# An mLSTM cell and a gated MLP on one core: gates of four chunks at once, and half passes in the second chunk

## The chip, the cores and the metric

The kernel runs on 1 core of one Trainium2 chip. The metric is the device time of one execution in microseconds (us), smaller is better. "TensorE" (PE in the profile) multiplies matrices, "VectorE" (DVE), "ScalarE" (ACT) and "GpSimd" (POOL) work element by element, and SP only issues transfers; ScalarE and GpSimd issue some as well. Each of them works off its own queue in order.

## The reference, cut to what matters

```python
# attention: batch 4, heads 8, sequence S = 768, head size D = 40
for t in range(S):
    m_new = np.maximum(f_gate[:, :, t] + m, i_gate[:, :, t])
    f_stab = np.exp(f_gate[:, :, t] + m - m_new)
    i_stab = np.exp(i_gate[:, :, t] - m_new)
    m = m_new
    C = f_stab[..., None, None] * C + i_stab[..., None, None] * outer(v_t, k_t)
    n = f_stab[..., None] * n + i_stab[..., None] * k_t
    y[:, :, t] = sigmoid(o_gate_t) * (C @ q_t) / np.maximum(np.abs(n @ q_t), 1.0)
# then an MLP on x = y as (3072, 320):  w_in (320, 2048), w_out (2048, 320)
h = x @ w_in
out = (h / (1 + np.exp(-1.702 * h))) @ w_out
```

All data are float32.

## The kernel before

**Chunks.** The sequence is cut into NW = 6 chunks (w = 0 to 5) of L = 128 steps. A chunk's attention works on all 32 pairs of batch and head (BH) at once; its result is 512 rows (4 batches x 128 steps) of 320 features for the MLP. The program is one stream of calls in a hand-made order: for each w an *up* stage (x @ w_in in 8 pairs j of 128-wide feature blocks), then a *down* stage (the product with w_out), into which the attention of chunk w + 1 is woven block by block (`attention`, the dictionary `side`). A pool's tag with `bufs` buffers hands them out in turn; a tile that takes a buffer waits for whoever still uses it.

**The gates.** `gates(w)` runs on VectorE, on 32 partitions: a running sum of f, a running maximum, and what has to be exponentiated later, with the two halves of the chunk swapped for odd heads by the masks `odd` and `even`. Each chunk starts from the maximum that the chunk before left (`m_at`). `load_gates` (two loads) comes before it; `gates_out` stores the results to DRAM in five transfers, `columns_in` fetches them back in five as columns, and `spread` fetches the running maximum once for all 128 partitions into two `wt` tiles. `side_queue` says who issues: GpSimd for chunk 1, SP for the others. `gates(1)` stands in the up stage of chunk 0 after pair j = 3, `gates(2)` in that of chunk 1 after j = 0, the later ones in down stages (i == 7).

**The up stage and its terms.** From chunk 1 on, a float32 product is made of rounded parts: `x_high`, `x_low`, `x_diff` against `w_high`, `w_low`, `w_diff`, for the first 256 features (k = 0, 1), in two sums, `main` and `side`. The last 64 features are in `x_rest` and `w_rest`. In chunks 2 to 5 `up_strips` does this in half passes: `halves` gives two matmuls of 64 rows each, one for each block of the pair, on the two halves of the array, so that both run together. There the last 64 features take one term `both` (high and low parts on the two halves) and one `strip`, half as much. A half pass that would write a sum while its other half is still on its way waits for a mark: `seen` puts an empty instruction into ScalarE's queue that waits for a matmul, and the next matmul waits for it. Chunk 1 uses `up_fast`: whole passes of 128 rows, eight terms for each block, two of them for the last 64 features, and no marks.

**Around it.** `evict_side` (ScalarE) and `evict_main` (VectorE) empty the sums, `gelu_fast` (ScalarE) follows. During the up stage of chunk 1 the parts of w_in that the later chunks need are also made (`split_high` on ScalarE, `split_diff` and `split_low` on VectorE) and stored to DRAM by `keep`, on ScalarE's queue. `keep_last` copies the last of them to another buffer. `weight_sums`, `hidden_difference` and `hidden_sums` (GpSimd, the last two pairs on VectorE) prepare the down stage, which from chunk 1 on takes seven products of sums instead of eight. `half_sums` and `wait_for` (a one-column copy to `mark`) hold GpSimd back until a given tile is written. `count` adds increments of a semaphore that nobody waits for to the first `COUNTS[w]` passes of a stage.

Of the kernel before, what the change touches and what calls it, by code (L numbers as in the profile page):

```python
# [8 lines left out]
FP = mybir.dt.float32  # L9
# [16 lines left out]
COUNTS = {0: 54, 1: 128, 2: 105, 3: 105}  # L26
# [9 lines left out]
def kernel(  # L36
# [178 lines left out]
    one1 = const.tile([BH, 1], FP, name="one1")  # L215
# [3 lines left out]
    ones = one1.to_broadcast([BH, L])  # L219
# [9 lines left out]
    odd, even = (const.tile([3 * BH, 1], FP, name=n) for n in ("odd", "even"))  # L229
# [10 lines left out]
    cols, stacked, m_row, raw = {}, {}, {}, {}  # L240
# [61 lines left out]
    def gates(w):  # L302
# [30 lines left out]
        if w:  # L333
            for x in range(2):
                V.tensor_scalar(out=swapped[:, x * HL:(x + 1) * HL], in0=st[:, (1 - x) * HL:(2 - x) * HL], scalar1=odd,
                                scalar2=None, op0=OP.mult)
            V.scalar_tensor_tensor(out=swapped, in0=st, scalar=even, in1=swapped, op0=OP.mult, op1=OP.add)
# [4 lines left out]

    def gates_out(w):
        m_run, swapped, both = stacked[w]
        to = m_row[w] = rows.tile([2, BH, HL], FP, name="m_row")
        side_queue(w).dma_start(out=to[:, 0::2].rearrange("n h t -> h n t"),
                          in_=m_run[0::2].rearrange("h (n t) -> h n t", t=HL))
        for n in range(2):
            side_queue(w).dma_start(out=to[1 - n, 1::2], in_=m_run[1::2, n * HL:(n + 1) * HL])
        st_row = rows.tile([L // 32, 3 * BH, 32], FP, name="st_row")  # L350
        d_row = rows.tile([BH, 2], FP, name="d_row")
        stacked[w] = st_row, d_row
        side_queue(w).dma_start(out=st_row.rearrange("n k t -> k n t"), in_=swapped.rearrange("k (n t) -> k n t", t=32))
        side_queue(w).dma_start(out=d_row, in_=both)
# [11 lines left out]
    def masks():  # L366
        V.tensor_reduce(out=odd, in_=full.rearrange("p (j two) -> p two j", two=2)[:, 1], axis=AX.X, op=OP.add)
        V.memset(odd[BH:2 * BH, :], 0.0)
        V.tensor_scalar(out=even, in0=odd, scalar1=-1.0, scalar2=1.0, op0=OP.mult, op1=OP.add)

    def columns_in(w):
# [3 lines left out]
        for n in range(L // 32):  # L375
            side_queue(w).dma_start(out=x[n * 32:n * 32 + 32, 0:3 * BH].rearrange("r (k t) -> r k t", t=32),
                              in_=st_row[n].rearrange("(k r) t -> r k t", r=BH))
# [46 lines left out]
    def spread(w):  # L424

        for c in range(2):
# [281 lines left out]
    w_high, w_low, w_diff, w_rest = {}, {}, {}, []  # L708
# [11 lines left out]
    def by_strips(w):  # L720
        return w > 1

    def rooms(w):
# [4 lines left out]
        if w > 1:  # L728
            w_low.update({(w, n): gp.tile([128, 2, 512], FR, tag="g", name="w_low")
                          for n in ((2, 3) if by_strips(w) else (2,))})  # L730
# [4 lines left out]
    def more_rooms(w):  # L735

        w_low[w, 3], w_diff[w, 2], w_low[w, 2], w_diff[w, 3] = (gp.tile([128, 2, 512], FR, tag="g", name=name)
                                                                for name in ("w_low", "w_diff", "w_low", "w_diff"))
# [18 lines left out]
    def keep_last():  # L757
        w_low[3] = work.tile([128, 2, 512], FR, tag="wx", bufs=1, name="w_low")
        A.copy(out=w_low[3], in_=w_low.pop((1, 3)))

# [15 lines left out]

    def strip_weights():

        wr = w_rest[0]
        w_rest.append(work.tile([128, NF // 2, 128], FR, tag="wx", bufs=1, name="w_strip"))  # L780
        d, low, high = w_rest[1], wr[64:128], wr[0:64]
# [12 lines left out]
    def split_x(w, c):  # L794
# [9 lines left out]
        A.activation(out=x_rest[w][0][:, t], in_=x[:, 2], func=AF.Copy, scale=BIAS if by_strips(w) else -BIAS / BASE)  # L804
# [9 lines left out]
    def split_x_rest(w, c):  # L814
        t, x = part_of(w, c)
        both, other = x_rest[w]
        if by_strips(w):
            V.scalar_tensor_tensor(out=other[:, t], in0=both[:, t], scalar=-1.0 - 1.0 / BASE, in1=x[:, 2], op0=OP.mult,
                                   op1=OP.add)
        else:  # L820
            V.scalar_tensor_tensor(out=other[:, t], in0=x[:, 2], scalar=-1.0 / BASE, in1=both[:, t], op0=OP.mult,
                                   op1=OP.subtract)
# [6 lines left out]
    def split_on(w):  # L829
# [5 lines left out]
        if by_strips(w):  # L835
# [12 lines left out]
    def up_fast(w, j):  # L848
# [33 lines left out]
        if j:  # L882
            gelu_fast(w, j - 1)
# [535 lines left out]
```

## Time and profile before

| | us |
|---|---|
| median of 3 runs | 438.51 (437.26 to 439.23) |
| the profiled execution | 438.98 |
| its span in the profile | 437.3 |
| TensorE busy | 431.9 |
| VectorE busy | 353.5 |
| ScalarE busy | 247.2 |
| GpSimd busy | 146.7 |

The granted clock of TensorE is 1.00 throughout. A line of the timeline has the start, the duration, the engine, the line of the kernel, the operation, output and inputs with their sizes, how many instructions are merged, and in brackets how long the engine had stood idle and what ended that. In the chain of waits each line is the start, the length and what the chain was then in.

### The profile page before, as it was taken

The page shows a single profiled execution, that of the slowest core. Times are in us where ns is not written, and L with a number is a line of the kernel's source. Part 1 is how long each engine was busy: PE and PEld are TensorE (multiplying, and loading weights), DVE is VectorE, ACT ScalarE, POOL GpSimd, SP SyncE. Part 2 cuts the span into 40 slices and gives each one's busy share as a digit, 9 for nine tenths or more (in the row PEclk, how much of TensorE's full clock was granted, in tenths as well). Part 3 has the DMA queues.
Part 4 walks back from the last instruction along what each step waited for, and adds up shares of the span by engine and source line. Part 5 has one row for each costly group of instructions (what it writes and reads, how often), then busy time and mean ns, then how long its engine had stood idle before and what let it go on. Part 6 is the DMA issues. An engine that isn't in the chain of part 4 may idle for free.

```text
span 437.3 us, 13451 instructions
## 1 busy us (share of the span) xinstructions
PE 431.9 (99%) x5342; PEld 375.0 (86%) x5342; DVE 353.5 (81%) x689; ACT 247.2 (57%) x540; POOL 146.7 (34%) x155
## 2 busy tenths in 40 slices
PE   8999999999999999999999999999999999999996
PEld 6877887777888999888999888999887999888996
DVE  4898998989889799659789659789759759779990
ACT  5677779922777900397900386900287940298720
POOL 6411326533056822035712035622036624013100
PEclk9999999999999999999999999999999999999999
DMA  8999999217797516999306997605998925820000
GB/s 169 188 285 193 254 252 225 66 34 186 198 206 152 127 49 156 312 161 172 54 31 146 311 178 154 86 19 131 282 197 151 121 66 125 258 98 2 0 32 30
DMA packets 130733, 64.07 MB, mean 147 GB/s; under 512 B 102208, under 2 KB 122672, under 8 KB 130672
## 3 DMA queue, kind: packets, MB, share of 16 engines
q1 hardware_dynamic: 121232, 57.48, 59.4%
q10 hardware_dynamic: 8768, 4.28, 3.4%
q0 software_dynamic: 672, 1.46, 1.2%
q8 instruction: 43, 0.70, 0.7%
q14 instruction: 18, 0.15, 0.1%
HBM read 51.86 MB, written 11.34 MB: 145 GB/s over the span
## 4 chain that ended last, share of the span: by engine, by line
PE 94%; ACT 2%; DVE 1%; DMA 1%; issue 0%; SPq 0%; DVEq 0%
PE p_out L1036 26%; PE p_h L911 13%; PE p L911 10%; PE p_out L979 8%; PE p_h L663 7%; PE p L1114 5%; PE p L865 3%; PE p_h L865 3%; PE p L931 3%; PE p L540 2%; PE p L548 2%; PE p L496 2%; PE p_h L673 2%; PE p_out L1114 2%; PE p L639 2%; PE p L412 1%
## 5 line engine op out<-in xcount | busy, mean ns | idle before, releaser
L803 ACT ACTIVATE x_high<-xT 128x512 fp32r<-128x512 f32 x10 | 6.3, 631 | 88.4 <-DVE xT L609 88.4
L1036 PE MATMUL p_out<-w_out,g 128*128 128x160 f32 x384 | 55.5, 301 | 0.0
L1036 PEld LDWEIGHTS p_out<-w_out,g 128*128 128x128 f32 x384 | 52.9, 190 | 1.6 <-ACT g L966 1.3
L843 ACT ACTIVATE g<-g 128x512 f32<-128x512 f32 x80 | 45.7, 629 | 1.9 <-DVE g L971 1.6
L1004 POOL TENSOR_TENSOR g<-g 128x512 f32<-128x512 f32 x16 | 20.5, 1302 | 69.9 <-ACT g L843 63.1
L971 DVE SCALAR_TENSOR_TENSOR g<-p,g 128x512 f32<-128x512 f32 x40 | 25.7, 684 | 22.5 <-PE p L911 19.2
L966 ACT ACTIVATE g<-p 128x512 f32<-128x512 f32 x40 | 21.7, 596 | 34.9 <-PE p L911 29.8
L469 ACT ACTIVATE wt<-wt,cols 128x64 f32<-128x64 f32 x160 | 38.9, 335 | 0.1
L1036 PE MATMUL p_out<-t_sb,s 128*128 128x160 f32 x256 | 37.8, 301 | 0.0
L1036 PEld LDWEIGHTS p_out<-t_sb,s 128*128 128x128 f32 x256 | 35.5, 190 | 0.2
L979 PE MATMUL p_out<-w_out,g 128*128 128x320 f32 x128 | 35.7, 436 | 0.0
L971 DVE SCALAR_TENSOR_TENSOR g<-p_h,g 128x512 f32<-128x512 f32 x40 | 25.7, 687 | 11.9 <-PE p_h L911 11.9
L979 PEld LDWEIGHTS p_out<-w_out,g 128*128 128x128 f32 x128 | 24.0, 190 | 9.5
L1021 POOL TENSOR_TENSOR s<-g,s 128x256 f32<-128x256 f32 x16 | 12.9, 835 | 52.8 <-PE p_out L1036 52.8
L663 PE MATMUL p_h<-xT,w_in 128*128 128x256 f32 x128 | 29.8, 385 | 0.1
L663 PEld LDWEIGHTS p_h<-xT,w_in 128*128 128x128 f32 x128 | 23.6, 190 | 5.4 <-issue 2.2
L966 ACT ACTIVATE g<-p_h 128x512 f32<-128x512 f32 x40 | 21.6, 593 | 10.3 <-PE p_h L911 9.2
L476 POOL TENSOR_SCALAR_AFFINE_SELECT wt<-wt 64x1024 f32<-64x1024 f32 x20 | 24.3, 1214 | 6.9 <-ACT wt L469 6.0
L625 POOL TENSOR_TENSOR vw<-v_st,cols 128x656 f32<-128x656 f32 (+1 forms) x13 | 16.7, 1301 | 25.0 <-PE p_out L1036 15.4
L1041 DVE TENSOR_TENSOR o_sb<-o_sb,p_out 128x160 f32<-128x160 f32 x56 | 16.3, 314 | 9.7 <-PE p_out L1036 9.2
L421 DVE STREAM_TRANSPOSE qT<-q_sq 128x512 f32<-128x512 f32 x20 | 20.4, 1109 | 1.2 <-ACT q_sq L122 1.2
L911 PE MATMUL p_h<-x_diff,w_diff 64*128 64x512 f32 x128 | 20.3, 395 | 0.0
(260 smaller groups left out, 1097.2 us busy)
## 6 DMA issues: line engine op xcount, KB each, us to landing
w_diff<-w_row SPq DMA_DIRECT2D x16, 512.0 KB, 4.8
wt<-m_row SPq DMA_DIRECT2D x20, 256.0 KB, 5.3
bits<-in_moe_w_in_dram SPq DMA_DIRECT2D x8, 512.0 KB, 9.5
w_low<-w_row SPq DMA_DIRECT2D x8, 512.0 KB, 6.2
out_dram<-o_sb SPq DMA_DIRECT2D x24, 160.0 KB, 2.9
q_sq<-in_q_dram SPq DMA_DIRECT2D x10, 320.0 KB, 8.1
eo<-in_o_gate_dram SPq DMA_DIRECT2D x5, 640.0 KB, 7.4
bits<-in_moe_w_out_dram SPq DMA_DIRECT2D x8, 320.0 KB, 5.4
```

What stands on the lines that cost most here:

```text
L469: A.activation(out=x[:, h, :], in_=x[:, h, :], func=AF.Exp, scale=-1.0, bias=cols[w][:, c * PH + h:c * PH + h + 1])
L476: G.affine_select(out=r, in_=r, compare_op=OP.is_ge, fill=0.0, base=0, pattern=[[0, PH], [1, HL]], channel_multiplier=-1)
L663: T.matmul(ph[j][i][:, t], w_in[f // 4][:, c, f % 4 * 128:f % 4 * 128 + 128], x[:, c, t], start=(first and c == 0 and n == 0), stop=(not f ...
L843: A.activation(out=g, in_=g, func=AF.Gelu_apprx_sigmoid)
L865: T.matmul(dst[i], a(i), x, start=(first and m == which[0]), stop=(last and m == which[-1]))
L911: mm = T.matmul(to[f], a(f)[r], x[r], start=(first and n == 0), stop=(last and n + 1 == len(parts)))
L966: A.activation(out=g[:, i, :], in_=opened[w, j][0][i], func=AF.Copy, scale=-BASE)
L971: V.scalar_tensor_tensor(out=g[:, i, :], in0=opened[w, j][1][i], scalar=1.0 + 1.0 / BASE, in1=g[:, i, :], op0=OP.mult, op1=OP.add)
L979: T.matmul(po, gs[w, f // 2][:, f % 2, b * L:(b + 1) * L], w_out_sb[f // NH][:, f % NH, :], start=(f == 0), stop=(f == NF - 1))
L1004: G.tensor_tensor(out=a10, in0=a00, in1=a10, op=OP.subtract)
L1036: T.matmul(po, a(f), b[:, f, :], start=(f == 0), stop=(f == NH - 1))
L1114: T.matmul((main, side, main)[n], g_part[n, b, f // 2][:, f % 2], wo[n, f][0][:, wo[n, f][1]], start=(f == order[0] and n < 2), stop=(f == ...
```

## The change

The gates of chunks 1 to 4 are loaded together into one tile of 128 partitions by eight loads in GpSimd's queue (`load_four`, during the attention of chunk 0), and worked out together on VectorE where `gates(1)` stood (`gates_four`); the maximum is carried from one chunk to the next in four one-column steps. GpSimd stores chunk 1's results, SP stores those of chunks 2 to 4 in the down stage of chunk 0 (`four_out`). `gates` is left for chunk 0 and chunk 5. Chunk 1's up stage becomes `up_strips`, with marks of GpSimd in pairs 0 to 4 and of ScalarE afterwards. Its `strip` weights are made on VectorE before the stage (`first_strip`, in a `wt` buffer), `x_rest` gets one more step on VectorE, the gelus come later, the last `w_low` gets a buffer of the pool `sp` and is stored by ScalarE's queue without the copy, and the second half of chunk 2's `spread` comes after pair 7. `COUNTS[1]` goes from 128 to 154, and products of the down stage are counted too.

```diff
-COUNTS = {0: 54, 1: 128, 2: 105, 3: 105}
+COUNTS = {0: 54, 1: 154, 2: 105, 3: 105}
...
+    def load_four():
+        x = work.tile([L, 768], FP, tag="y", name="gates4")
+        four["in"] = [x[:, n * L:(n + 1) * L] for n in range(4)]
+        for n, src in enumerate((f_gate, i_gate)):
+            for x in range(4):
+                G.dma_start(out=four["in"][n][x * BH:(x + 1) * BH],
+                                  in_=src[:, :, (x + 1) * L:(x + 2) * L].rearrange("b h s -> (b h) s"))
+
+    def gates_four():
+        f, i, f_run, m_run = four["in"]
+        x = work.tile([L, 768], FP, tag="y", name="gates4")
...
+        V.tensor_tensor_scan(out=f_run, data0=ones4, data1=f, initial=0.0, op0=OP.mult, op1=OP.add)
+        V.tensor_tensor(out=a, in0=i, in1=f_run, op=OP.subtract)
+        V.tensor_tensor_scan(out=m_run, data0=ones4, data1=a, initial=NEG, op0=OP.mult, op1=OP.max)
+        V.tensor_copy(out=m[0:BH], in_=m_at[1])
+        for n in range(4):
+            r = slice(n * BH, (n + 1) * BH)
+            V.scalar_tensor_tensor(out=m[(n + 1) * BH:(n + 2) * BH] if n < 3 else m_at[NW - 1], in0=m_run[r, L - 1:L],
+                                   scalar=m[r], in1=f_run[r, L - 1:L], op0=OP.max, op1=OP.add)
+        V.tensor_scalar(out=m_run, in0=m_run, scalar1=m, scalar2=None, op0=OP.max)
...
-        w_low[w, 3], w_diff[w, 2], w_low[w, 2], w_diff[w, 3] = (gp.tile([128, 2, 512], FR, tag="g", name=name)
-                                                                for name in ("w_low", "w_diff", "w_low", "w_diff"))
+        w_low[w, 3] = sp.tile([128, 2, 512], FR, tag="g", name="w_low")
+        w_diff[w, 2], w_low[w, 2], w_diff[w, 3] = (gp.tile([128, 2, 512], FR, tag="g", name=name)
+                                                   for name in ("w_diff", "w_low", "w_diff"))
...
+    def first_strip():
+        w_strip[1] = work.tile([128, NF // 2, 128], FR, tag="wt", bufs=2, name="w_strip")
+        V.scalar_tensor_tensor(out=w_strip[1], in0=rest_high, scalar=-1.0 / BASE, in1=rest_low, op0=OP.mult, op1=OP.add)
...
-        if by_strips(w):
-            both, other = x_rest[w]
-            V.scalar_tensor_tensor(out=both[64:128], in0=other[64:128], scalar=BASE, in1=both[64:128], op0=OP.mult,
-                                   op1=OP.add)
+        both, other = x_rest[w]
+        V.scalar_tensor_tensor(out=both[64:128], in0=other[64:128], scalar=BASE, in1=both[64:128], op0=OP.mult, op1=OP.add)
...
-        note = (A if w + 1 < NW else nc.sync).nop()
+        note = (nc.sync if w + 1 == NW else G if w == 1 and j < 5 else A).nop()
...
-        late = j < 3 and w + 1 < NW
-        for n in ((), (), (0, 1))[j] if late else (j - 1,) if w + 1 < NW or j + 1 < NF // 2 else ():
+        late = {1: (), 2: (), 3: (0, 1), 4: (2,), 5: (3,), 6: (4, 5)} if w == 1 else {1: (), 2: (0, 1)} if w + 1 < NW else {7: ()}
+        for n in late.get(j, (j - 1,)):
...
+    load_four()
+    load(1, "k")
...
-                    gates(1)
-                    gates_out(1)
+                    gates_four()
+                    four_out(G, 1, 2)
...
-                (up_strips if by_strips(w) else up_fast)(w, j)
+                up_strips(w, j)
...
                     if j == 2:
-                        split_high(3)
                         keep(w_diff_row, 2, w_diff[1, 2])
                         keep(w_low_row, 2, w_low[1, 2])
+                    if j == 3:
                         split_diff(3)
                         split_low(3, V)
-                        sums_from = w_low[1, 3].bitcast(FP)[:, 0, :]
-                    if j == 3:
                         keep(w_diff_row, 3, w_diff[1, 3])
-                        keep_last()
-                        wait_for(sums_from)
+                        keep(w_low_row, 3, w_low[1, 3])
+                    if j == 4:
+                        wait_for(w_low[1, 3].bitcast(FP)[:, 0, :])
                         weight_sums(2)
-                    if j == 5:
-                        keep(w_low_row, 3, w_low[3], nc.sync)
...
-                    spread(w + 1)
+                    spread(w + 1, range(1 if w == 1 else 2))
...
+                if w == 1 and j == 7:
+                    spread(2, (1,))
...
-                lag = 3 if w == 1 else 2
+                lag = 4 if w == 1 else 2
...
+            if w == 0 and i == 3:
+                four_out(nc.sync, 2, NW - 1)
...
                 split_low(0, V)
+                first_strip()
```

`split_high(3)` moves to after the filling of the squares in pair 2, and `up_fast`, `by_strips` and `keep_last` are gone.

## The prediction

> **What bounds the kernel now.** I read the page first: busy times, then the chain that ended last.
>
> ```profile
> span 437.3 us, 13451 instructions
> ...
> PE 431.9 (99%) x5342; PEld 375.0 (86%) x5342; DVE 353.5 (81%) x689; ACT 247.2 (57%) x540; POOL 146.7 (34%) x155
> ...
> PE 94%; ACT 2%; DVE 1%; DMA 1%; issue 0%; SPq 0%; DVEq 0%
> ```
>
> TensorE is idle for 5.4 us in all, nearly all of it at the two ends of the span. Work taken from another engine saves nothing; only fewer passes on TensorE do, and anything that comes too late for TensorE costs. So I compare the stretch that the change rewrites, the up stage of chunk 1, with the same stage of chunk 2, which already runs the new code (busy time in stretches, TensorE alone):
>
> ```profile
> 108.54:138.00 29.46, 29.46 (x131) 1.00 0.78 191
> 176.90:204.71 27.81, 27.81 (x229) 1.00 0.99 207
> ```
>
> The columns are length, TensorE busy with its matmul count, granted clock, DMA share, GB/s. Both stretches are full, one is 1.65 shorter. Next, what comes due at the edges, by the chain of waits:
>
> ```profile
> 31.29 1.92 PE p_h L673 x8
> ...
> 151.02 0.51 DVE state L648
> 151.53 0.04 issue
> 151.58 1.16 PE p L496 x64
> ...
> 176.90 2.76 PE p L931 x12
> 179.67 0.89 PE p_h L911 x6
> ```
>
> At 151.58 TensorE waits for VectorE: the only place inside the span where it is near a wait. Then the timelines of VectorE, ScalarE and GpSimd, for prices and slack:
>
> ```profile
> 30.21 0.69 DVE L285 CUSTOM_DVE_ANT_0 w_in_x<-bits,w_in_x 128x1024 uint16<-128x1024 uint16 x1
> 51.22 1.01 DVE L284 TENSOR_SCALAR bits<-bits 128x512 uint16<-128x512 uint16 x1
> 99.46 1.22 DVE L745 SCALAR_TENSOR_TENSOR w_diff<-w_high,w_in 128x1024 fp32r<-128x1024 f32 x1
> 178.49 0.69 DVE L837 SCALAR_TENSOR_TENSOR x_rest<-x_rest 64x512 fp32r<-64x512 f32 x1
> ```
>
> ```profile
> 49.29 1.65 POOL L349 DMA_DIRECT2D m_row<-m_run  x2
> 137.29 1.29 POOL L1015 TENSOR_TENSOR s<-s,g 128x512 f32<-128x512 f32 x1
> 142.37 2.75 POOL L625 TENSOR_TENSOR vw<-v_st,cols 128x656 f32<-128x656 f32 x2 [3.79 <-PE p_out L1036]
> ```
>
> **1. Half passes in chunk 1.** Before, each of 8 pairs of feature blocks takes 8 terms x 2 passes = 16, 128 in all: 29.46 / 128 = 0.230 each. After, a couple of 64-row half passes counts as one: 17 in the first pair (12 whole, 5 couples), 16 in the second, 15 in each of the next five, 12 in the last: 120. By passes that is 8 x 0.230 = 1.84; by chunk 2, whose stage is the same code, 29.46 - 27.81 = **1.65**. I take 1.65 and keep 1.84 as the bound: the difference of 0.19 is what entering and leaving half passes costs. At the entry itself nothing shows: 12 whole passes from 176.90 take 2.76 and the next starts at 179.67, 0.01 later.
>
> The Trainium skill, page "TensorEngine Tiling (Array Packing)", section Tiling Modes, says that a change of tiling mode drains TensorE. By it the two changes would cost this stage something beyond the passes; the two rows show at most 0.19 for them together, and it lies inside the 1.65.
>
> The 100 more matmul instructions (229 against 131 in the stage) and 26 more semaphore increments on TensorE cost nothing: chunk 4, with none of the increments, has the same stage in 27.80 (310.76 to 338.56).
>
> **2. Loading four chunks of gates.** Eight issues on GpSimd, put behind its copy at 24.77. Its issue rows run from 0.55 to 0.83 (the two L349 took 1.65 together), so about 5.5: 25 to 31. Queued behind them is the mark at 35.32, which had waited 10.31: no cost there. VectorE slows beside such issues: L284 takes 1.01 and 0.85 beside ten of them, against its usual 0.74, with 0.4 in all; 0.3 for eight. That would hit the conversion that ends at 30.90 (30.21 + 0.69) and that TensorE needs at 31.29: slack 0.39. I book 0; without that slack 0.3. SP loses two issues there (0.33, 0.32), a gain that nothing waits for.
>
> **3. gates_four on VectorE.** The old block runs from 46.66 to 50.44, 3.78. The new one, by the old rows: the free sizes are mostly the same; added are a copy and four one-column steps minus one (4 x 0.15), one 128-wide maximum (0.28), and twice the width in three selecting steps (about 0.3): 1.1 more. Behind it is the conversion that ended at 52.88 and that TensorE reads from 55.94 on: slack 3; VectorE also idles 0.42, 0.66 and 1.22 before 75.36. Cost 0. GpSimd's ten issues for chunk 1 are as many as before, 1.1 later; its columns are read by ScalarE at 68.28 and delays there have 3.3 of slack (transposes end at 79.15, scores start at 82.47). On SP, five issues of about 0.6 for chunks 2 to 4 replace two gate loads that held it from 69.98 to 75.95; its next is at 94.81. Cost 0. The VectorE blocks and seven SP issues each that chunks 2 to 4 lose gain 0: TensorE is full there (25.00 of 25.00 between 152 and 177).
>
> **4. Splits before chunk 1.** VectorE gets the strip (as L745, 1.2) and one more step on x_rest (as L837, 0.69). Idle times of 0.26, 0.32 and 0.19 take in 0.77 of the first, so x_low comes 0.45 later, at about 108.4, and TensorE wants it after six passes, at 109.93. x_rest comes at about 110.6 and is wanted at 112.2. If GpSimd's half sums slow the strip (L616 took 1.02 beside GpSimd against 0.50), 0.5 more: still covered. The load of k_sq, issued at 105.32, waits for the strip to be read at about 103.0: no delay. Cost 0, bound 0.4.
>
> **5. Evictions and marks inside the stage.** I lined up ScalarE and VectorE by the durations of chunk 2 (eviction pair 0.96, gelu pair 1.05, table 1.28, VectorE pair 1.2, transposes 2.0). The tight place is the fourth pair: ScalarE must wait for VectorE's split of the last weights (about 126.7) before it can issue their two stores, and the fifth eviction stands behind them, done at about 127.8; TensorE wants that bank at about 128.1. From then on the marks are ScalarE's again, behind the same queue. GpSimd's marks: its queue is empty from 106.5 to 124.8 (then it waited 18.29), and it started 0.14 after VectorE at 124.80 and 0.31 at 48.60; TensorE has five couples (1.15) between the work marked and the work that waits. ScalarE loses the copy of the last weights (1.05), and the store of w_low moves from SP's queue to its own. Moved too: half of chunk 2's spread now waits on SP for the strip's buffer, which TensorE leaves at about 132.2; with 5.3 to land it is there at 138, and ScalarE comes to it at about 145. Behind it on SP is only the load of the output gates, which waits for the stage's end in any case. Cost 0.1; bounds 0 and 0.8.
>
> **6. The seam to chunk 2.** TensorE ends the stage at about 136.2 (108.55 + 27.7). GpSimd's last sum ended at 138.58. Its chain (2.9 for weight sums, four differences, four sums of 1.3) now starts 1.9 later, at 126.7, and also waits for the later gelus: about 140.3. Its next work, the scaled values, started 4.4 after TensorE's stage end; that is now 140.6. Cost 0.15; bounds -0.1 (the wait at 151.5 vanishes) and 2.
>
> **Sum.** -1.65 + 0.1 + 0.15 = -1.4. The profiled execution took 438.98 (span 437.3 and 1.68 around it): it would be 437.6. The median of the runs shown is 0.47 lower, 438.51: I predict **437.1**. About 0.5% (2.2 us) is what a measurement of this kernel can tell from no change; the three runs alone lie 1.97 apart.
>
> **Rivals.** (a) More is kept: 1.84, the wait at 151.5 gone, shorter queues: 436.4. For it speaks that SP and VectorE are relieved in four chunks; against, that none of this is waited for. (b) ScalarE's queue or the marks eat the gain: one eviction 0.5 late at the fourth pair is passed on through the next two: 1.0 to 1.9 lost, 438.5. For it: 0.3 of slack at one place. Against: ScalarE was idle 1.26 and 1.80 late in the same stage of chunk 2. In the case that GpSimd's marks are slow, nine marks 0.2 past their cover give 1.8 too. (c) The slower side: GpSimd becomes the bound at the seam. If the last weights' buffer, now shared with the first difference that ScalarE's queue stores (5.9 to land, one such store 8.6), is free late, VectorE splits late, the weight sums start late, and values, decay, masks and then the scores at 151.58 move one for one. It decides from 0.3 late and undoes the gain from 2.0; 2 to 4.5 late is 439 to 441.5, say 440.2. Against: the store is issued near 116, ten before the buffer is wanted. (d) The gates come too late.
>
> The Trainium skill, "SBUF — State Buffer", section Who interferes with whom, says that GpSimd and some VectorE instructions shut each other out of a shared pair of ports, with its descriptors for DMA among what waits. By it the loads at 25 to 31, where VectorE is busy 4.67 of 5.00, would be late; the trace shows a pair of such issues stretched to 1.65 and none beyond.
>
> Gate loads took up to 10.7 to land; by 41 they are there, 5.7 before 46.7, and TensorE has 3 more. Rival (d) would need 9 late, and then cost what is over: 438 to 441.
>
> **Chances.** Forecast 0.48 (436.7 to 437.6), (a) 0.14, (b) 0.24, (c) 0.11, (d) 0.03. Faster by over 0.5% is below 436.3: a third of (a), and the runs' scatter on the forecast: 0.17. Slower is above 440.7: some of (c) and (d), and what I have not seen: 0.12. Within: 0.71. The range leaves out the upper half of (c) and the edge of (a): 435.9 to 440.0.
>
> **What would show it.** Right: the up stage of chunk 1 takes 27.6 to 28.0 with about 229 matmuls, and TensorE stays full. Wrong in 2: L673 starts after 31.4. In 4: a gap at 109 to 112. In 5: TensorE idle on ScalarE's evictions between 127 and 131. In 6: the scores of chunk 2 start later than 15.4 after the stage's end.

## The result

The changed kernel takes 441.66 us (median of 6 runs, 440.56 to 442.79), the kernel before 438.63 in the same comparison: a ratio of 1.0071 (95% interval 1.0046 to 1.0096), some 3.0 us slower where 1.4 less was forecast. The profiled execution, the fastest of the six, took 440.56 against 438.98, so 1.6 of the 3.0 can be read in the traces.

First the page, by its busy times and by the head of the chain that ended last:

```profile
span 438.8 us, 13658 instructions
...
PE 431.1 (98%) x5442; PEld 372.2 (85%) x5442; DVE 349.5 (80%) x658; ACT 246.9 (56%) x539; POOL 154.1 (35%) x163
...
PE 13%; DMA 2%; DVE 0%; ACTq 0%; SPq 0%; issue 0%; DVEq 0%
```

TensorE has 0.8 less work, and its idle time went from 5.4 to 7.7. The chain was 94% TensorE and ran through the whole span; now it breaks off at 365.76, in a stretch of transfers. The stretches that answer to those shown of before (length, then busy time and instructions of TensorE, its weight loads, VectorE, ScalarE and GpSimd, granted clock, DMA share, GB/s):

```profile
108.11:136.45 28.34, 28.18 (x230) 22.21 (x229) 25.59 (x33) 21.27 (x38) 9.25 (x7) 1.00 0.98 246
...
376.79:427.97 51.18, 50.15 (x374) 43.27 (x374) 45.21 (x93) 32.65 (x72) 7.81 (x8) 1.00 0.18 61
```

The up stage of chunk 1 is 28.34 with 230 matmuls, from 29.46 with 131: 1.12 is saved. The second row, chunk 5 up to its last products, has 1.03 in which TensorE does nothing. Its own timeline shows every wait that the change brought:

```profile
30.76 1.13 PE L730 MATMUL p_h<-xT,w_in_x 64*128 64x512 f32 x4
...
128.02 0.73 PE L923 MATMUL p<-x_diff,w_diff 64*128 64x512 f32 x4 [0.17 <-ACT g L981]
...
149.56 1.16 PE L553 MATMUL p<-qT,kT 40*64 40x64 f32 x64 [0.60 <-DVE state L705]
151.03 1.16 PE L553 MATMUL p<-qT,kT 40*64 40x64 f32 x64 [0.32 <-DVE state L705]
...
378.96 0.74 PE L945 MATMUL p<-x_diff,w_diff 128*128 128x512 f32 x2 [0.99 <-DVE x_diff L866]
```

L730 (L673 before) starts at 30.76, which is 5.71 after the first matmul of chunk 0's up stage; before it was 5.71 too (31.22 by the timeline). So the eight loads hold nothing up there. The scores of chunk 2 wait 0.92 for VectorE, and chunk 5 begins with a wait of 0.99 that the kernel before does not have.

Measured from the first matmul of a stage to the first of the next, in us of the profiled executions (e5 to e15 are experiments, below):

| | before | changed | e5 | e9 | e14 | e15 |
|---|---|---|---|---|---|---|
| up to the up stage of chunk 0 | 25.51 | 25.05 | 24.74 | 25.20 | 24.30 | 25.85 |
| chunk 0, both stages | 82.64 | 82.67 | 82.85 | 83.42 | 82.69 | 82.64 |
| up stage of chunk 1 | 29.65 | 28.52 | 28.57 | 28.35 | 28.55 | 29.65 |
| down stage of chunk 1 | 38.84 | 39.85 | 39.87 | 38.89 | 39.83 | 38.92 |
| chunks 2 to 4 | 200.52 | 200.71 | 200.68 | 200.72 | 200.86 | 200.49 |
| chunk 5 to its last products | 49.39 | 51.18 | 49.20 | 49.22 | 49.20 | 51.35 |
| the rest | 10.72 | 10.87 | 10.87 | 10.86 | 10.87 | 10.73 |

Two places eat the gain and more: the seam from chunk 1 to chunk 2 (+1.01) and the last seam, from chunk 4 to chunk 5 (+1.79).

### The profile page after: what moved, and what is told of

It is laid out like the page before. It is cut to its first block, busy times and chain, and to the rows that moved or that the text cites. A ratio compares the mean times of both kernels' runs of the same rounds, so it can differ in the third digit from the quotient of the medians.

```text
span 438.8 us, 13658 instructions
## 1 busy us (share of the span) xinstructions
PE 431.1 (98%) x5442; PEld 372.2 (85%) x5442; DVE 349.5 (80%) x658; ACT 246.9 (56%) x539; POOL 154.1 (35%) x163
## 5 line engine op out<-in xcount | busy, mean ns | idle before, releaser
L923 PE MATMUL p_h<-x_diff,w_diff 64*128 64x512 f32 x160 | 25.3, 394 | 0.0
L923 PE MATMUL p_h<-x_low,w_low 64*128 64x512 f32 x160 | 25.0, 390 | 0.0
L923 PE MATMUL p_h<-x_high,w_high 64*128 64x512 f32 x160 | 24.9, 389 | 0.0
```

The costliest lines, as they stand in the source:

```text
L923: mm = T.matmul(to[f], a(f)[r], x[r], start=(first and n == 0), stop=(last and n + 1 == len(parts)))
```

## The experiments

**The halves of the change, and the seam's first test.** a2 is the changed kernel again, e1 has only the half passes, e2 only the gates of four chunks. e3 changes one thing at the seam to chunk 2:

```diff
-                if j >= 6:
+                if j == 6 or j == 7 and w > 1:
                     hidden_sums(w, (j - 6,), G)
...
-                hidden_sums(w, (2, 3), V)
+                hidden_sums(w, (1, 2, 3) if w == 1 else (2, 3), V)
```

> The changed kernel once more, unchanged. In its first profile TensorE was idle for 0.60 and 0.32 us ahead of the scores of chunk 2 (waiting for VectorE's states) and 0.99 ahead of the first differences of chunk 5 (waiting for x_rest, whose stores on ScalarE's queue took 4.4 us to land instead of 2.3), and the two matmuls groups around that place lost about another 1.0. Theory 1 (both losses belong to the change): both come again, 0.9 at the first place within 0.2 and 1.5 to 2.0 at the last seam; median 441 to 442.5 beside 438.6. Theory 2 (the last seam was chance in a transfer that varies): the first loss comes again, at the last seam TensorE starts chunk 5 within 0.5 of what the kernel before shows, and the span of the profiled execution is near 437.3. Theory 3 (both chance): neither comes again, 437.3 to 438.

Measured: 441.97, ratio 1.0088 (1.0054 to 1.0122). The waits ahead of the scores came again (0.43 and 0.31), and at the head of chunk 5 TensorE waited 0.57, its stretch 50.85. Both losses belong to the change.

> Only the half passes of chunk 1 with all that belongs to them (strip, splits, marks on GpSimd, order of splits and spreads); the gates are loaded and computed chunk by chunk as before, so the block of gates for chunk 2 (3.8 us on VectorE) stays inside the up stage of chunk 1. The up stage should fall from 29.46 to about 28.5 as in the changed kernel (theory A, the passes and the seam are all of the loss: GpSimd's chain of sums ends at about 140.8 as there or later, TensorE idles 0.9 or more ahead of the scores of chunk 2, and the last seam is as before, so about 438.6). By theory B (the half passes also squeeze VectorE, which has 3.8 more to do here) the last splits come 2 to 3 later, evictions stand behind them, TensorE idles 1 to 3 inside the stage: 440 to 441.5. By theory C (the loss at the last seam comes with the half passes and not with the gates) chunk 5 starts 1.5 to 2 late as well: 440 to 443.

Measured: 445.77, ratio 1.0162 (1.0146 to 1.0178). TensorE waits 1.45 and 2.69 inside the up stage, which takes 34.41: theory B, with a larger price than expected. Not all of the price is waiting: the stage is 5.9 longer than in the changed kernel, the waits are 4.1 of it, and over the stage the mean granted clock is 0.95 (1.00 in the changed kernel), which is worth 1.7. So the half passes need the gates out of that stage, which is what the other half of the change does for them. Chunk 5 takes 51.19: the loss of the last seam comes with the half passes (C).

> Only the gates of four chunks at once; chunk 1 keeps its 128 whole passes and its old order, without the block of gates for chunk 2 in its up stage. Theory A (the gates are covered everywhere and the loss is at the seam behind the half passes): GpSimd's sums end before 138.6 as before, no wait of TensorE ahead of the scores of chunk 2 above 0.1, the last seam as before: 438.0 to 438.8. Theory C (the new layout of the small DRAM tiles or the changed loads of the gates block carry the loss at the last seam): chunk 5 starts 1.5 to 2 late, TensorE idle about 1.0 ahead of the first x_diff matmul of chunk 5: 440 to 441.5.

Measured: 438.97, ratio 1.0022 (1.0006 to 1.0037), every stretch within 0.08 of the kernel before, but for the head (0.51 shorter) and the rest behind chunk 5 (0.14 longer). In the profile the gates are covered, and neither loss is theirs. The interval still leaves out no change at all: by it the gates cost 0.3 to 1.6 us, of which the profiled run shows only the 0.14 at the end.

> The changed kernel with one edit: in chunk 1 GpSimd keeps one of its two hidden sums and VectorE does three instead of two, so GpSimd is done at about 138.0 instead of 140.8. Theory A (the two engines slow each other when both run two-input steps on SBUF: VectorE's four steps took 6.69 beside GpSimd against 2.69 in the kernel before): VectorE's six steps take 1.35 a pair of steps, 4.1, with some slowing by the scaled values from 140.7 on, end by 143.3 instead of 144.7, the states come 0.9 earlier and the two waits of 0.60 and 0.32 ahead of the scores vanish: 0.6 to 0.9 less than the changed kernel. Rival (VectorE is simply late, by its own amount of work): a third sum adds 1.3, its steps end at 146, TensorE waits 2 instead of 0.9: 1 more than the changed kernel. Nothing at the last seam changes.

Measured: 440.83; of the two waits one of 0.43 is left, the down stage of chunk 1 takes 39.43 instead of 39.85. VectorE's first three sums, now with GpSimd idle beside them, took 1.84 together (0.61 each); in the changed kernel two took 3.22. The next three took 4.07: the first, begun before GpSimd's scaled values (140.82), 0.67, and the two beside them 1.77 each. More work on VectorE made it earlier, so it is the company that slows it, not its amount.

**The seam to chunk 2, again.** e8 moves GpSimd's weight sums forward, in two halves:

```diff
         note = seen(w, j, halves(sums, 0, first=True))
+        if w == 1 and j == 3:
+            weight_sums(2, slice(0, NH // 2))
...
             notes.append(seen(w, j, ahead))
+        if w == 1 and j == 3:
+            weight_sums(2, slice(NH // 2, NH))
...
-                    if j == 4:
-                        wait_for(w_low[1, 3].bitcast(FP)[:, 0, :])
-                        weight_sums(2)
```

> The changed kernel with one edit: GpSimd's weight sums (2.97 us in one instruction behind the split of the last weights) are done in two halves between the marks of the fourth pair, at about 120 to 123.5, while VectorE does evictions out of PSUM and transposes. GpSimd's chain of hidden sums then ends at about 138 instead of 140.8. Theory A (two-input steps of both engines on SBUF slow each other): VectorE's four hidden sums take 2.5 to 3.3 instead of 6.69, no wait of TensorE ahead of the scores of chunk 2 above 0.1, 0.8 to 1.0 less at this seam. In the same places: VectorE's evictions and transposes beside the halves keep their 0.65 and 1.0. Rival (the marks behind the halves come late): TensorE waits 0.3 to 1.5 inside the fourth and fifth pair, and the gain at the seam is gone.

Measured: 440.74, the same down stage (39.87), VectorE's four steps 6.74. The edit did not do what it was to do: GpSimd then stood idle 3.63 ahead of its first hidden sum, which needs the gelu of pair 4, and that gelu now comes after pair 6. VectorE's evictions out of PSUM (0.64 each) and transposes (1.03) beside the two halves kept their times.

**The last seam: what crowds what.** There, ScalarE's queue stores the second half of x (`x_row`, `x_rest`), SP loads it back (`q_sq`), and GpSimd loads 640 KB of `w_out`. The chain of the changed kernel shows the slow part:

```profile
367.10 4.23 DMA x_rest<-y
...
372.02 5.46 DMA q_sq<-x_rest
...
378.58 0.34 DVE x_diff L866
378.92 0.04 issue
378.96 2.52 PE p L945 x8
```

The store took 4.23 to land, then the load 5.46, during which the first packets of `w_out` were moving (from 373.1 on). e5 holds `w_out` back:

```diff
     def fetch_w01():
+        wait_for(x_square(1, 1)[:, 0])
         G.dma_start(out=w01, in_=w01_row[0])
```

> The changed kernel with one edit: at the last seam GpSimd's 640 KB load of w_out waits until the second x_rest loads have landed; in the changed kernel its packets begin at 372.9, in the middle of those loads, which then take 5.5 us to land. Theory W (the large load takes the DMA engines from the small one, and that is what makes x_rest late): the x_rest loads land within 3 us of their issue, TensorE's wait of 0.6 to 1.1 at the head of chunk 5 is gone or below 0.2, 1.2 to 2.0 less than the changed kernel, even where the store on ScalarE's queue is slow. Rival (the slow store alone does it): the loads are issued 0.6 late as before, and at least half of the loss of 1.8 stays. If w_out is needed early in chunk 5, its parts come late and TensorE or ScalarE waits there: slower by up to 3.

Measured: 438.76, ratio 0.9991 (0.9959 to 1.0023), 2.9 less than the changed kernel's 441.66. (The 441.66 is from another session; the ratios, each to the kernel before measured beside it, are 0.9991 and 1.0071.) Chunk 5 takes 49.20 and TensorE does not wait, although ScalarE's store was as late as ever (last packet 5.63 after the first issue). Theory W: what costs the time is `w_out` among the x_rest loads. Why the store is late is another question. The change also moved one transfer to ScalarE's queue; e4 moves it back, e6 moves it in the kernel before:

```diff
-                        keep(w_low_row, 3, w_low[1, 3])
...
+                    if j == 5:
+                        keep(w_low_row, 3, w_low[1, 3], nc.sync)
```

```diff
-                        keep(w_low_row, 3, w_low[3], nc.sync)
+                        keep(w_low_row, 3, w_low[3])
```

> The changed kernel with one edit: the store of the last low weights goes back to SP's queue behind the sixth pair, as in the kernel before, so that ScalarE's queue has issued 22 transfers and not 23 ahead of the last seam. Seen so far: in the four profiles with the half passes ScalarE's last x_rest store ends 3.3 to 4.1 us after its issue there, in the two without them 1.5 and 1.7. Theory Q (how many transfers ScalarE's queue has issued decides how its packets of the last seam fall): the store ends within 2 us of its issue, the loads behind it come 0.5 to 1 earlier, TensorE does not wait ahead of the first x_diff matmul of chunk 5, 1.5 to 2.0 less than the changed kernel. Rival S (other consequences of the half passes, as the rotation of buffers, make the store slow): it ends 3.3 or more after its issue again, TensorE waits 0.5 to 1.1 there, time as the changed kernel's. The waits ahead of the scores of chunk 2 stay (0.9).

> The kernel before with one edit: the store of the last low weights is issued on ScalarE's queue and not on SP's, one transfer more on that queue ahead of the last seam and nothing else. Theory Q (the count of transfers on that queue decides): ScalarE's last x_rest store now ends 3.3 or more after its issue, and chunk 5 starts up to 2 late: 439.5 to 440.7. Rival S (it comes with the half passes): the store ends within 2 us as in the kernel before, and the time is that of the kernel before within 0.4, 438.3 to 439.0.

Measured: e4 441.26, last packet 5.01 after the first issue, chunk 5 51.49; e6 438.77, 4.18 and 49.41. Theory Q falls twice. (In e4 the up stage of chunk 1 took 28.35 instead of 28.52, without the wait of 0.17.)

**Why is the store late?** e11 puts four small copies between ScalarE's first and second store of the last seam:

```diff
                     in_=ys[w, c][:, b, at:at + g * m].rearrange("t (g y) -> t g y", y=m))
+                if w + 1 == NW and c == 1 and g == 4 and b == 0:
+                    for _ in range(4):
+                        A.copy(out=pause, in_=one1)
```

> The changed kernel with one edit: four copies of one column on ScalarE, about 0.8 us, between its first and second x_row store at the last seam. In the three profiles without a loss there (the kernel before, with the store moved, and gates alone) the second store's issue took 1.10 to 1.25 and the last packet of ScalarE's stores ended 3.9 to 4.2 after the first issue; in the six with half passes in chunk 1 it took 0.46 and the last packet ended 4.9 to 5.8 after. Theory P (issuing close together is what makes the packets slow): with the pause the last packet ends within 4.3 of the first issue, the x_rest loads are issued 0.7 earlier and TensorE's wait of 0.6 to 1.5 at the head of chunk 5 shrinks below 0.3. Rival (the slow issue is only a sign of something else that the half passes change): the last packet ends 5.5 or more after, and the wait is as large or larger by up to 0.8.

Measured: 441.70, last packet 5.28, chunk 5 51.61. Not the spacing.

e12 gives the changed kernel the buffer places of the kernel before from chunk 2 on, e13 the other way round (`PLACES` lists, for each tile in its order, which of the 8 or 4 buffers it gets):

```diff
-    gp = ctx.enter_context(tc.tile_pool(name="gp", bufs=NH))
-    sp = ctx.enter_context(tc.tile_pool(name="sp", bufs=4))
+    gp = Placed([ctx.enter_context(tc.tile_pool(name=f"gp{n}", bufs=1)) for n in range(8)], PLACES["gp"])
+    sp = Placed([ctx.enter_context(tc.tile_pool(name=f"sp{n}", bufs=1)) for n in range(4)], PLACES["sp"])
```

> The changed kernel with one edit: the twelve shared buffers (eight for gelu's output, low weights and transposed x, four for sums and weight differences) are handed out so that from chunk 2 on each tile lies where it lies in the kernel before; nothing in the order of work changes. In the change, one tile moved from the one pool to the other, and so every later tile of both lies elsewhere; the transfers of the last seam and their own addresses are alike with and without the half passes. Theory L (where the tiles that the engines read and write at that time lie decides how fast the transfers beside them go): ScalarE's last x_rest packet ends at most 4.3 us after its first issue (4.9 to 5.8 in the changed kernel), TensorE's wait at the head of chunk 5 falls from 0.6 to 1.5 to below 0.2, and the up stages of chunks 2, 3 and 4 are 28.07, 28.24, 28.07 as before and not 28.25, 28.06, 28.25: 439 to 440. Rival M (places do not matter, something in the order or the timing of the work does): packets end 4.9 or later, the wait is there, time as the changed kernel's.

> The kernel before with one edit, the counterpart: its twelve shared buffers are handed out so that from chunk 2 on each tile lies where it lies in the changed kernel. Theory L: ScalarE's last x_rest packet ends 4.9 us or more after its first issue (3.9 to 4.2 in the kernel before), the load of w_out enters among the x_rest loads, TensorE waits 0.6 to 1.5 at the head of chunk 5, and the up stages of chunks 2 to 4 swap to 28.25, 28.06, 28.25: 440 to 441. Rival M: nothing changes, 438.2 to 439.2.

Measured: e12 442.40, last packet 5.63, chunk 5 51.97; e13 439.12, 4.89 and 49.43. The up stages of chunks 2 to 4 kept the pattern of their order of work, not of their places. Theory L falls: e12, with the old places, is as late as ever. In e13, though, the store ended late too (4.89, just under the 4.9 of the theory), and chunk 5 lost nothing, so a late store alone does not cost the time.

What did sort the profiles was the row of instruction blocks in the page's part on DMA queues. Between 368.0 and 369.5 the changed kernel has, by queue and kind, the packets, their MB and their share of the 16 DMA engines:

```profile
q10 hardware_dynamic: 959, 0.18, 62.4%
q1 hardware_dynamic: 260, 0.12, 36.6%
q8 instruction: 1, 0.02, 3.7%
q14 instruction: 1, 0.01, 1.8%
```

The q8 packet has 16384 bytes, and 3.7% of 16 engines over 1.5 us is one engine for 0.89. It comes at 368.45, in the middle of the packets of ScalarE's queue (q10). In the kernel before it comes at 365.95, when ScalarE's packets have not begun:

```profile
q1 hardware_dynamic: 50, 0.05, 20.9%
q8 instruction: 1, 0.02, 6.4%
x_row<-y ACTq DMA_DIRECT2D x2, 128.0 KB, 3.5
```

(between 365.7 and 366.7). Counted from ScalarE's first store, the block comes after 0.09 to 0.29 in the kernel before, e2, e6 and e13, and after 2.47 to 3.49 in the changed kernel, a2, e1, e3, e4, e5, e8, e9, e11 and e12. (The q14 block, 8192 bytes, does not sort them: e1 loses without one near, and e2 has one among the packets and loses nothing.) TensorE's queue has 10309 instructions up to chunk 5 in the kernel before and 10539 in the changed one (counted in the traces); the 230 more are 200 for the half passes, 26 for the larger `COUNTS[1]`, 4 others. In the trace of the kernel before, 256 of TensorE's instructions lie between one such block and the next, on average over its 43 blocks. If a block is 256 instructions, 26 more make the shift a whole block. e14 and e15 do that, and nothing else:

```diff
-COUNTS = {0: 54, 1: 154, 2: 105, 3: 105}
+COUNTS = {0: 54, 1: 154, 2: 105, 3: 131}
```

and in the kernel before

```diff
-COUNTS = {0: 54, 1: 128, 2: 105, 3: 105}
+COUNTS = {0: 54, 1: 128, 2: 105, 3: 79}
```

> The changed kernel with one edit: 26 more semaphore increments on TensorE's queue in chunk 3 (105 becomes 131). Up to chunk 5 the change adds 230 instructions to that queue (10539 against 10309 in the trace), and the blocks of 16 KB that the trace shows being fetched for it are 256 instructions each if one takes 64 bytes; 26 more make it a whole block, so that the fetches of the last seam should fall where they do in the kernel before. Theory F (the block fetched among the packets of ScalarE's store makes that store late): the fetch comes within 0.3 us of the store's first issue instead of 3.1 after it, the last packet ends 3.9 to 4.3 after that issue, TensorE's wait at the head of chunk 5 is gone, chunk 5's stage takes 49.4 instead of 51.2, 2 to 3 less than the changed kernel: 438.6 to 439.6. The 0.9 ahead of the scores of chunk 2 stays. Rival (the fetch is only a clock hand beside it): the stage takes 50.8 or more, time as the changed kernel's. If the 26 increments cost time, at most 26 x 0.03 = 0.8 in chunk 3.

> The kernel before with one edit: 26 semaphore increments fewer on TensorE's queue in chunk 3 (105 becomes 79), which puts the fetches of the last seam where the changed kernel has them. Theory F: the block is fetched 2.4 to 3.5 us after the first issue of ScalarE's store, its last packet ends 4.9 or more after that, the load of w_out enters among the x_rest loads, TensorE waits 0.6 to 1.7 at the head of chunk 5: 51 in that stage instead of 49.4, 1.5 to 3 slower than the kernel before, 440 to 441.7. Rival: nothing changes, 438.2 to 439.0.

Measured: e14 438.44, ratio to before 1.0007 (0.9985 to 1.0029), 3.2 less than the changed kernel's 441.66 (ratio 1.0071, measured apart); e15 441.35, ratio 1.0061 (1.0046 to 1.0076), 2.6 more than the kernel before. The block came 0.13 and 3.07 after the store, as theory F has it. The increments themselves cost little: chunk 3 takes 66.96 in e14 and 66.84 in the changed kernel. The transfers of the last seam (from 363 to 380; KB, median time to landing), e14 first, e15 second:

```profile
q_sq<-x_rest SPq DMA_DIRECT2D x4, 64.0 KB, 2.7
x_rest<-y ACTq DMA_DIRECT2D x2, 32.0 KB, 2.3
```

```profile
q_sq<-x_rest SPq DMA_DIRECT2D x4, 64.0 KB, 4.6
x_rest<-y ACTq DMA_DIRECT2D x2, 32.0 KB, 4.3
```

And TensorE in e15, the kernel before but for 26 increments, waits where the changed kernel waits:

```profile
379.67 0.73 PE L931 MATMUL p<-x_diff,w_diff 128*128 128x512 f32 x2 [0.92 <-DVE x_diff L811]
```

The page of e14 has its chain through the whole span again:

```profile
span 436.3 us, 13684 instructions
...
PE 94%; DMA 2%; ACT 2%; DVE 1%; issue 0%; SPq 0%; DVEq 0%; ACTq 0%
```

Step by step, in us:

| | before | changed | e5 | e13 | e14 | e15 |
|---|---|---|---|---|---|---|
| block, after the first issue of ScalarE's store | 0.19 | 3.07 | 3.38 | 0.29 | 0.13 | 3.07 |
| last packet of the store, after the same | 4.04 | 5.10 | 5.63 | 4.89 | 4.02 | 5.28 |
| first packet of `w_out`, after the issue of the last x_rest load | 3.63 | 1.04 | 4.85 | 1.61 | 3.56 | 1.17 |
| that load, issue to landing | 2.65 | 5.46 | 2.25 | 2.67 | 2.29 | 5.42 |
| chunk 5 to its last products | 49.39 | 51.18 | 49.20 | 49.43 | 49.20 | 51.35 |

So the position of a block of TensorE's code, moved by instructions that do no work, makes or removes the loss of the last seam, in either kernel. The loss needs `w_out` close behind the loads: e5 has the late store without it. And e13 shows that a store can also be late with the block early; why it is there stays open. Only these two positions of the block were set on purpose.

**Versions built on this.** e9 joins e5, e4's edit, e8 and an earlier gelu, with all four differences ahead of the sums; e16 adds the 26 increments.

```diff
-        late = {1: (), 2: (), 3: (0, 1), 4: (2,), 5: (3,), 6: (4, 5)} if w == 1 else {1: (), 2: (0, 1)} if w + 1 < NW else {7: ()}
+        late = {1: (), 2: (), 3: (0, 1), 4: (2,), 5: (3, 4), 6: (5,)} if w == 1 else {1: (), 2: (0, 1)} if w + 1 < NW else {7: ()}
...
-                if lag <= j < 4 + lag:
-                    hidden_difference(w, j - lag)
+                for n in {4: (0,), 5: (1,), 6: (2, 3)}.get(j, ()) if w == 1 else (j - lag,) if lag <= j < 4 + lag else ():
+                    hidden_difference(w, n)
```

> The changed kernel with what the runs so far point to: the load of w_out at the last seam waits for the x_rest loads (worth 2.0 in its profile); the store of the last low weights is SP's again behind the sixth pair (the up stage of chunk 1 was 0.2 shorter with it, 28.35); and at the seam to chunk 2 GpSimd gets out of VectorE's way: weight sums early, gelu of pair 4 already behind pair 5, all four differences ahead of the sums. Moving the weight sums alone did nothing (VectorE's four steps 6.74), since GpSimd then waited 3.63 for the gelu of pair 4. Theory A (two-input steps of both engines on SBUF slow each other): GpSimd's last sum ends at most 1.5 after TensorE's stage end (it was 4.6), VectorE's four hidden sums take 2.5 to 3.3, no wait above 0.1 ahead of the scores: down stage of chunk 1 38.9 instead of 39.85. Then chunk 5's stage 49.2, and in all 1.0 to 1.5 less than the kernel before: 437.2 to 437.7 where that has 438.7. Rival (the chain is VectorE's own): 39.4 or more in that stage, time that of the kernel before. If the earlier gelu holds up the eviction of the seventh pair, TensorE waits 0.2 to 0.4 there.

Measured: 438.51, ratio 0.9985 (0.9956 to 1.0014). At the seam theory A holds in full: VectorE's hidden sums in the changed kernel, then in e9:

```profile
138.16 3.22 DVE L1027 TENSOR_TENSOR s<-g 128x512 f32<-128x512 f32 x2
141.30 3.47 DVE L1030 TENSOR_TENSOR s<-s,g 128x512 f32<-128x512 f32 x2
```

```profile
138.88 1.35 DVE L1031 TENSOR_TENSOR s<-g 128x512 f32<-128x512 f32 x2
140.15 1.29 DVE L1034 TENSOR_TENSOR s<-s,g 128x512 f32<-128x512 f32 x2
```

The same four steps take 2.64 instead of 6.69. What stands beside them on GpSimd explains it, in the changed kernel and in e9:

```profile
137.88 1.27 POOL L1027 TENSOR_TENSOR s<-g 128x512 f32<-128x512 f32 x1
139.23 1.60 POOL L1030 TENSOR_TENSOR s<-s,g 128x512 f32<-128x512 f32 x1
140.78 3.44 POOL L682 TENSOR_TENSOR vw<-v_st,cols 128x656 f32<-128x656 f32 x2
```

```profile
137.08 1.29 POOL L1034 TENSOR_TENSOR s<-s,g 128x512 f32<-128x512 f32 x1
141.08 2.75 POOL L682 TENSOR_TENSOR vw<-v_st,cols 128x656 f32<-128x656 f32 x2 [2.72 <-PE p_out L1055]
```

In e9 GpSimd is done at 138.4, before VectorE begins, and the down stage is 38.89, as before the change.

> The best version so far (half passes, four gates at once, the w_out load behind x_rest, GpSimd out of VectorE's way at the seam to chunk 2, one store on SP's queue) with the 26 increments more in chunk 3. By theory F its last seam is then safe twice over: stage 49.2 to 49.4 and less scatter. By its stages it should be 1.2 (up stage of chunk 1, 28.35 against 29.65, the seam as before) better than the kernel before, 0.3 of that lost in chunks 2 and 4: 437.4 to 437.9 where that has 438.6. Rival (the gains are eaten elsewhere by the scatter of the first 100 us): 438.3 to 438.8.

Measured: 437.94, ratio 0.9989 (0.9969 to 1.0009). By its parts it should be 1.1 ahead of the kernel before (1.3 in the up stage of chunk 1, less 0.2 in chunks 2 to 4); the interval holds that and also nothing. Its profiled execution has the parts (28.34, 38.64 and 49.20 in the two stages of chunk 1 and in chunk 5), but chunk 0 takes 83.38 there and chunks 2 to 4 take 201.79, 0.7 and 1.3 more than before. Others have the like: e9 and e6 in chunk 0 (83.42, 83.14), a2 in chunk 3 (67.93 against 66.84 in the changed kernel). The cause stays open. A version that beats the kernel before is not shown.

## Why the prediction was wrong

**The failed step is the sentence in step 1 that the 100 more matmul instructions and the 26 more semaphore increments cost nothing.** Its argument was that chunk 4 has none of the increments and the same stage: true, and it looks only at the time that TensorE needs to issue them. What they also do is move every later block of TensorE's code against the rest of the program. At the last seam that puts a block among the packets of a store, the store is late, the loads behind it are late, and a load that does not wait for any of this enters among them. Cost: 1.8 in the profile, in a stage for which no step has a term. e14 takes back 3.2 in the median; that the median lost more than the profiled run fits a price that varies from run to run, but single runs without a profile do not show it.

**Step 6 had the delay right and its effect wrong.** It said that GpSimd's last sum would end at about 140.3; it ended at 140.83. It priced this at 0.15, by GpSimd's own next work. The price is 1.0, because VectorE's sums, which used to begin after GpSimd was done (140.10 against 138.58), now run beside it, and both slow down: VectorE's from 0.67 to 1.67 each. In the kernel before they were

```profile
140.10 1.41 DVE L1012 TENSOR_TENSOR s<-g 128x512 f32<-128x512 f32 x2
141.43 1.28 DVE L1015 TENSOR_TENSOR s<-s,g 128x512 f32<-128x512 f32 x2
```

The prediction had such a row in hand: step 4 cites L616, 1.02 beside GpSimd against 0.50, but for the strip and not for the sums. The 1.0 lies inside the step's own bound of 2, and the sign set for the step (scores later than 15.4 after the stage's end) was too wide to show it: the second half of the scores starts 14.8 after the first product of the down stage, 13.8 before.

Rival (c) named the right engine and the right stage, but its mechanism, late weights, did not occur; the weights were split at 126.5, as forecast.

**The gain of step 1** is 1.12 of the 1.65. Of the 0.53 that is missing, some 0.2 was never there: the stretch 108.54:138.00 ends 0.21 behind the first product of the down stage (137.79), while the one of chunk 2 ends on it (204.71). From the second matmul to that product chunk 1 took 29.17 before and chunk 2 takes 27.74, a difference of 1.43. (The second matmul comes 0.47 after the first in chunk 1, with and without the change, and 0.34 in chunk 2.) The other 0.31 is lost at the fifth pair (against the same passes of chunk 2 in e2), where step 5 put the tight place: the eviction behind the stores of the last weights, with a visible wait of 0.17 at 127.85, which is the sign that step 5 had set. The reading that nothing shows at the entry to half passes does not hold either: it sets the end of one row against the start of the next. From start to start the first couple comes 0.32 after the last whole pass and the second 0.33 after the first, where passes come 0.23 apart. These 0.19 are paid in chunk 2 too, so they lie inside the 1.65. Step 5 booked 0.1 with a bound of 0.8; e4, which takes one store off that queue, gains 0.17. **Steps 2, 3 and 4** held in the profiles: e2's stretches show the gates free, and no gap came at 109 to 112. Rival (d) is out with them.

So the sum of the steps, -1.4, becomes in the profile -1.13 (up stage) + 1.01 (seam) + 1.79 (last seam) + 0.19 (chunks 2 to 4) + 0.15 (tail, which e2 has too) - 0.43 (head and chunk 0) = 1.58. The 0.19 is 0.16 and 0.18 more in the up stages of chunks 2 and 4, 0.18 less in that of chunk 3, and 0.03 of rests; the pattern comes with the half passes in chunk 1, and its cause stays open.

The Trainium skill, "SBUF — State Buffer", section Who interferes with whom, says that a VectorE instruction with two SBUF inputs contends with a GpSimd instruction that reads SBUF, and that one with at most one SBUF input, outside its two-port modes, does not. The traces agree on both: 1.67 against 0.67 for the two-input sums, and the unchanged 0.64 of evictions out of PSUM in e8. The prediction used that section for the loads and not for the sums, where it would have spoken against the change.

The Trainium skill, "Runtime: NRT & Kernel Launch", section Instruction fetch mechanics, says that an engine's code comes in blocks of 16 KiB, 256 instructions, by a DMA queue of its own, and that the cost of crossing a boundary is mostly hidden. Size and count agree with the traces of TensorE (16384 bytes; 256 instructions from block to block; a shift of 26 completes 230 to 256). Hidden it is for TensorE itself, which shows no wait at a block; for the transfers beside it e14 and e15 show 2.0 in the stretch of chunk 5.

What stays open: how one block on one DMA engine for 0.9 to 1.0 holds a store's last packets up by 1.1 (the changed kernel against e14) or 1.2 (e15 against the kernel before). The trace does not say which engine carries which packet. It is also not clear why a block at the very start of the stores does no harm; there ScalarE's second store takes 1.1 to 1.3 to issue instead of 0.46.

## What to carry to other kernels

When a step is moved onto a stretch where another engine works, price its company, not only its own end: two engines that were busy one after the other can each become slower when they overlap. When the number of instructions on a long queue changes, compare when the blocks of code are fetched around the tight transfers of both profiles; a few empty instructions can put them back. And order a large load explicitly behind a small one that the critical engine waits for, so that chance does not decide: that one wait was worth as much as the padding.

## What the hardware showed that was not expected

- 26 semaphore increments that do nothing moved a block fetch of 16384 bytes by 2.9 us against the transfers beside it, and with it the time of the whole kernel by 2.6 (e15) and 3.2 (e14) in opposite directions.
- A load of 640 KB whose packets begin 1.0 us after a load of 64 KB was issued goes with 5.46 us to landing for the small one; where they begin 1.6 us after (e13) or 3.6 us after (the kernel before), it is 2.67 and 2.65.
- VectorE's sum of two 128x512 tiles takes 0.64 to 0.69 alone and 1.54 to 1.77 beside GpSimd's steps; GpSimd's takes 1.30 alone, and 1.27 and 1.60 beside VectorE's.
